# A linear-attention, soft-mixture and feed-forward kernel on one core: power table by ScalarE, query-key products on GpSimd, a shorter warm-up, and a new order of all units of the first stage

## The chip, the core and the metric

The kernel runs on one core of a Trainium2 chip. The metric is the device time in microseconds (us) of one execution. The engines named below are TensorE (PE in the profile, with PEld for its weight loads), VectorE (DVE), ScalarE (ACT), GpSimd (POOL) and SyncE (SP), which issues every DMA of this kernel.

## The reference

Three stages follow one another. The first is a recurrent linear attention over 768 steps, for 4 batches and 8 heads of width 48:

```
cur   = (u * k_t) outer v_t
y_t   = r_t @ (state + cur)
state = w * state + k_t outer v_t
```

The second is a soft mixture of experts on x of shape (3072, 384): logits = x @ phi (32 slots); a softmax over all tokens builds the slot inputs d.T @ x; eight experts apply relu(s @ w1[e]) @ w2[e] to four slots each; a softmax over the slots mixes the results back to the tokens. The third is a feed-forward layer on the result, relu(x @ w_in) squared, times w_out, with a hidden width of 2048. All values are float32; w_in and w_out arrive as 64-bit floats and are turned to 32 bits on the chip.

## The kernel before

The attention is done in 16 units. Unit n is batch n // 4 and a pair of heads n % 4; its 768 steps are six chunks of 128. Five buffers of 128 x 3072 hold the units (unit n lies in buffer n % 5); `load_unit(n)` fetches unit n once the unit five before it has been read for the last time.

Per unit, these steps are written, each a small helper:

- `decay(n, m)`: VectorE multiplies keys (m = 1) or queries (m = 0) by powers of w from a table `tabp` that lies in PSUM. EV and OD, a third argument in places, are the even and odd chunks.
- `turns(x, k)`: TensorE transposes for the keys of unit k (ScalarE copies them out to `kn`) and for the output of unit x.
- `A(n, par)`: TensorE products of keys and queries within the even or odd chunks, into two of three PSUM banks with the tag "A" (for unit 0 and par = 1, one of them is the bank `pp`).
- the diagonal of those products: for units 0 to 2 by `rk(n)` (key times query, on GpSimd) and `dg_of(n)` (TensorE sums), for later units by `pr1`, `pr2` (GpSimd) and `weigh` (VectorE). `diag` (GpSimd) spreads the diagonal into a tile, and `cp` (VectorE, two copies) puts the lower triangle of A beside it, which frees the two banks.
- `KV(n)`, `scan(n)`, `inter(n)`, `intra(n, par)`: the state of each chunk, its running sum (VectorE), and the two parts of the output. `L(n)` makes the logits, and `soft1a` to `soft4`, `both` and `c_max` to `c_div` are the softmax work of each batch.

The order of all these units is written out by hand as one list of some 380 calls, and each engine works through its own instructions in that order. So the list also fixes the order in SyncE's queue: an issue that waits holds up all issues behind it. Among the calls are the loads of the second stage's weights. `load_piece(j)` loads a third (512 KB) of one of the first eight weight matrices: w1 of experts 0 to 5, then w2 of experts 0 and 1; pieces 21 to 23 are w2 of expert 1. `load_weight(8)` to `(13)` load a whole matrix (1536 KB) into a buffer that the attention gives up: 8 to 11 need the buffers of units 11 to 14, 12 that of unit 15, 13 the buffer of `scan` and `kn`. `load_win(0)` loads the first quarter of w_in into the buffer that holds `xn` of batches 0 and 2, which `soft3(2)` reads last.

Ahead of the list stand the loads of units 0 to 4, six `keep_clock` calls on TensorE (12 matmul instructions with no result that is used), and the making of the table: VectorE copies w, squares it five times, takes reciprocals of the six powers in one instruction, and doubles the table six times. `filler(2)` is two more unused TensorE products.

Behind the list come the softmax of the last batch, the experts (`ups(a)` and `downs(a)`, two experts each; each `up` takes a bank with the tag "A"), and between them, on VectorE, the conversion of w_in and w_out: `conv_some` works on the quarters 0 and 1 of w_in once `ups(1)` has given up its buffer, and `wout_f32` works on w_out. VectorE then copies out parts of `soT`, with which the third stage begins. That stage's main loop is at line 1251.

Of the kernel before, what the change touches and what calls it, by code (L numbers as in the profile page):

```python
# [17 lines left out]
def rwkv_softmoe_ffn(ctx: ExitStack, tc: tile.TileContext, un, wt, ph, w1, w2, w_in, w_out, out):  # L18
# [185 lines left out]
    tabp = ps("tab")[:112].rearrange("p (a e) -> p a e", a=NP)  # L204
    neg, pos = pw[:, 0], pw[:, 1]
    nc.vector.memset(tabp[:, :, 64:65], 1.0)
    nc.vector.tensor_copy(pos[:, 0], base[:, :NP])
    for i in range(5):
        nc.vector.tensor_mul(pos[:, i + 1], pos[:, i], pos[:, i])
    nc.vector.reciprocal(neg[:, :6], pos[:, :6])  # L210
    nc.vector.tensor_copy(tabp[:, :, 63:64], neg[:, 0].unsqueeze(2))
    for i in range(6):
        n = 1 << i
        blk = tabp[:, :, 64 - 2 * n:64 + 2 * n].rearrange("p a (q x) -> p a q x", q=4)
        by = pw[:, :, i].rearrange("p s a -> p a s").unsqueeze(3).to_broadcast([112, NP, 2, n])
        nc.vector.tensor_tensor(blk[:, :, 0::3], blk[:, :, 1:3], by, ALU.mult)
# [273 lines left out]
    def rsc_of():  # L490
        nc.vector.tensor_tensor(rsc, tabp, uw.unsqueeze(2).to_broadcast([112, NP, 128]), ALU.mult)
# [6 lines left out]
    def carry_of():  # L498
        nc.scalar.copy(carry[:, :, :, 1:], pos[:, 7].unsqueeze(2).unsqueeze(3).to_broadcast([112, NP, D, NC - 1]))
# [7 lines left out]
    def load_piece(j):  # L507
        load_weight(pieces[j][0], pieces[j][1:])
# [5 lines left out]
    def constants():  # L514
        nc.vector.reduce_sum(sel, ident.rearrange("p (q s) -> p s q", q=4).unsqueeze(1).to_broadcast([128, 4, NS, 4]), axis=AX.X)
        nc.vector.reduce_sum(rm, ident.rearrange("p (q e j) -> p e q j", q=4, e=E), axis=AX.XY)
        nc.gpsimd.memset(ones, 1.0)

    decay(0, 1, EV)
    load_piece(10)  # L520
    decay(0, 1, OD)
    carry_of()
    decay(0, 0, EV)
    rk(0, EV)
    decay(0, 0, OD)
    rk(0, OD, nc.vector)
    filler(2)
    turns(None, 0)
    A(0, 0)
    decay(1, 1)  # L530
    A(0, 1)
    KV(0)
    dg_of(0)
    diag(0, 1)
    filler(2)
    rsc_of()
    filler(2)
    decay(1, 0)
    filler(2)
    filler(2)  # L540
# [24 lines left out]
    decay(3, 0)
    cp(1, 1)
    diag(1, 0)
    cp(1, 0)
    load_unit(5)
    inter(1)  # L570
    KV(2)
    scan(2)
    pr1(3)
    intra(1, 0)
    constants()
    intra(1, 1)
    dg_of(2)
    diag(2, 0)
    load_unit(6)
    A(2, 0)  # L580
    turns(0, 3)
    load_piece(7)
    decay(4, 0)
    L(0)
    A(2, 1)
    cp(2, 0)
    inter(2)
    intra(2, 0)
# [24 lines left out]
    cp(3, 1)
    L(2)
    decay(5, 0)
    A(4, 0)
    inter(3)
    KV(4)
    weigh(4)
    diag(4, 0)  # L620
    decay(6, 1)
    scan(4)
    cp(4, 0)
    load_piece(3)
    intra(3, 0)
    intra(3, 1)
    A(4, 1)
    turns(3, 6)
    L(3)
    soft1d(0)  # L630
    pr2(5)
    weigh(5)
    diag(4, 1)
    A(5, 0)
    cp(4, 1)
    load_piece(15)
    diag(5, 0)
    pr1(6)
    decay(7, 1)
    cp(5, 0)  # L640
    pr2(6)
    load_unit(8)
    soft1a(0)
    soft1b(0)
    load_piece(4)
    inter(4)
    diag(5, 1)
    decay(7, 0)
    KV(5)
    scan(5)  # L650
    intra(4, 0)
    intra(4, 1)
    load_unit(9)
    A(5, 1)
    cp(5, 1)
    turns(4, 7)
    load_piece(17)
    pr1(7)
    weigh(6)
    decay(8, 0)  # L660
    both(0)
    c_max(0)
    A(6, 0)
    inter(5)
    intra(5, 0)
    diag(6, 0)
    cp(6, 0)
    KV(6)
    c_sub(0)
    diag(6, 1)  # L670
    load_piece(14)
    pr2(7)
    intra(5, 1)
    load_unit(10)
    decay(8, 1)
    A(6, 1)
    load_piece(2)
    turns(5, 8)
    load_piece(6)
    pr1(8)  # L680
# [20 lines left out]
    A(7, 1)
    turns(6, 9)
    L(6)
    weigh(8)
    A(8, 0)
# [12 lines left out]
    c_exp(0)
    intra(7, 1)
    decay(10, 0)  # L720
    c_sum(0)
    A(8, 1)
    cp(8, 1)
    weigh(9)
    load_piece(16)
    turns(7, 10)
    load_piece(0)
    L(7)
    A(9, 0)
    soft1a(1)  # L730
    inter(8)
    soft1b(1)
    KV(9)
    load_unit(12)
    decay(11, 1)
    load_piece(18)
    intra(8, 0)
    intra(8, 1)
    scan(9)
    KV(10)  # L740
    pr1(10)
    pr2(10)
    load_piece(11)
    diag(9, 0)
# [34 lines left out]
    inter(10)
    load_piece(22)  # L780
    intra(10, 0)
    pr2(12)
    intra(10, 1)
# [4 lines left out]
    soft1d(1)
    weigh(11)
    diag(11, 0)  # L790
    diag(11, 1)
    decay(13, 1)
    load_piece(19)
    cp(11, 0)
    decay(13, 0)
    load_piece(20)
    load_piece(9)
    cp(11, 1)
    load_weight(8)
    decay(12, 0)  # L800
    decay(14, 1)
# [3 lines left out]
    L(10)
    pr1(13)
    scan(12)
    inter(11)
    A(12, 0)
    pr2(13)  # L810
    intra(11, 0)
    weigh(12)
    diag(12, 0)
    diag(12, 1)
    KV(13)
    weigh(13)
    intra(11, 1)
    cp(12, 0)
    A(12, 1)
    turns(11, 14)  # L820
    decay(14, 0)
    L(11)
    cp(12, 1)
    load_weight(9)
    soft1a(2)
    A(13, 0)
    inter(12)
    intra(12, 0)
    pr1(14)
    intra(12, 1)  # L830
    soft1c(2)
    scan(13)
    load_weight(10)
    A(13, 1)
    diag(13, 0)
    decay(15, 1)
    soft1b(2)
    pr2(14)
    turns(12, 15)
# [10 lines left out]
    pr2(15)  # L850
    cp(13, 1)
    intra(13, 1)
    cp(14, 0)
    c_sub(1)
    KV(14)
    A(14, 1)
    turns(13, None)
    soft1d(2)
    load_weight(11)
    scan(14)  # L860
    decay(15, 0)
    c_exp(1)
    L(12)
    diag(14, 1)
    soft3(2)
    inter(14)
    A(15, 0)
    intra(14, 0)
    cp(14, 1)
    intra(14, 1)  # L870
    KV(15)
    A(15, 1)
    weigh(15)
    soft4(0)
    soft4(1)
    soft4(2)
    load_weight(13)
# [6 lines left out]
    cp(15, 0)
    diag(15, 1)
    scan(15)
    L(13)
    cp(15, 1)
# [434 lines left out]
```

## Time and profile before

| | us |
|---|---|
| median of 3 runs (373.4 to 373.82) | 373.75 |
| the profiled execution | 374.71 |
| its span, from the first to the last instruction | 373.0 |
| TensorE busy in that span | 365.9 (98%) |
| VectorE busy | 266.4 (71%) |
| ScalarE busy | 206.9 (55%) |
| GpSimd busy | 103.1 (28%) |
| chain of work that ended last, TensorE's share | 96% |

The attention takes the span up to about 113 us, the softmax of the last batch and the experts up to about 144 us, and the feed-forward layer the rest. A busy share is an average over all of these.

### The profile page before, as it was taken

The numbers are of one execution on the slowest core, as the hardware profiler recorded it, in microseconds if no ns is written. First come the engines' busy times: TensorE is split into PE (matmuls) and PEld (weight loads), VectorE is DVE, ScalarE is ACT, GpSimd is POOL, SyncE is SP. The second block draws the span as 40 slices with busy tenths as digits, with TensorE's granted clock in tenths as the row PEclk, the third lists the DMA queues.
The fourth block names the chain that finished last, engine by engine and source line by source line (L and its number), as shares of the span: only waits on it lengthen the run. The fifth ranks groups of instructions, "written<-read, shape, count | busy, mean of one in ns | idle before, by whom it ended". The sixth has DMA issues, their size and how long they took to land.

```text
span 373.0 us, 9092 instructions
## 1 busy us (share of the span) xinstructions
PE 365.9 (98%) x3716; PEld 297.8 (80%) x3716; DVE 266.4 (71%) x459; ACT 206.9 (55%) x447; POOL 103.1 (28%) x117
## 2 busy tenths in 40 slices
PE   8999999999999999999999999999999999999995
PEld 6888878887987556787878888888888888888884
DVE  7979878878673695999785767556666766556663
ACT  3234534544445344988887765555555655555553
POOL 4658795595734131352222400000000000000000
PEclk9999999999999999999999999999999999999999
DMA  7999899999999998333322003000000220000004
GB/s 251 405 377 415 294 401 386 390 372 393 317 397 410 386 417 293 94 112 94 106 93 65 7 38 131 2 1 0 3 0 0 88 84 0 2 1 0 2 0 169
DMA packets 22665, 65.22 MB, mean 175 GB/s; under 512 B 2544, under 2 KB 4832, under 8 KB 22624
## 3 DMA queue, kind: packets, MB, share of 16 engines
q1 hardware_dynamic: 22624, 64.65, 46.6%
q8 instruction: 29, 0.48, 0.5%
q14 instruction: 12, 0.10, 0.1%
HBM read 59.00 MB, written 4.72 MB: 171 GB/s over the span
## 4 chain that ended last, share of the span: by engine, by line
PE 96%; ACT 1%; DVE 1%; issue 1%; POOL 0%; POOLq 0%; ACTq 0%
PE ps_A L1251 26%; PE ps_tab L1251 9%; PE ps_kv L1251 9%; PE ps_lg L1251 9%; PE ps_A L311 7%; PE ps_YO L341 3%; PE ps_YE L350 3%; PE ps_YO L1138 3%; PE ps_A L952 3%; PE ps_YO L350 3%; PE ps_tab L973 3%; PE ps_YE L1138 3%; PE ps_lg L364 2%; PE ps_kv L323 2%; PE ps_YE L274 2%; PE ps_lg L227 1%
## 5 line engine op out<-in xcount | busy, mean ns | idle before, releaser
L1162 DVE TENSOR_TENSOR slot<-slot,slot 128x512 fp32r<-128x512 f32 (+1 forms) x97 | 70.2, 725 | 53.8 <-PE ps_A L1251 18.5
L1251 PE MATMUL ps_A<-slot,slot 128*128 128x512 f32 x429 | 105.3, 389 | 0.0
L1251 PEld LDWEIGHTS ps_A<-slot,slot 128*128 128x128 f32 x429 | 80.4, 188 | 16.8 <-DVE slot L1162 0.2
L1159 ACT CAST slot<-slot 128x512 fp32r<-128x512 f32 x95 | 58.9, 620 | 49.2 <-DVE slot L1156 48.9
L1156 DVE TENSOR_TENSOR slot<-slot 128x512 f32<-128x512 f32 x69 | 47.6, 691 | 11.4 <-ACT slot L1149 11.2
L1251 PE MATMUL ps_tab<-slot,slot 128*128 128x512 f32 x144 | 55.6, 393 | 0.1
L1251 PE MATMUL ps_kv<-slot,slot 128*128 128x512 f32 x144 | 55.1, 390 | 0.0
L1251 PE MATMUL ps_lg<-slot,slot 128*128 128x512 f32 x144 | 55.1, 389 | 0.0
L316 DVE COPY_PREDICATED AT<-mask,ps_A 128x384 f32<-128x384 int32 x63 | 33.5, 584 | 8.5 <-PE ps_A L311 3.2
L1149 ACT ACTIVATE slot<-ps_YO 128x512 f32<-128x512 f32 (+1 forms) x49 | 28.8, 589 | 12.8 <-PE ps_YO L1138 12.3
L1149 ACT ACTIVATE slot<-ps_YE 128x512 f32<-128x512 f32 x48 | 28.7, 598 | 12.3 <-PE ps_YE L1138 11.7
L1017 POOL TENSOR_TENSOR slot<-wf,slot 128x384 fp32r<-128x384 f32 x16 | 19.9, 1246 | 52.8 <-ACT slot L1012 52.8
L300 POOL TENSOR_SCALAR_AFFINE_SELECT AT<-dg 128x768 f32<-128x768 f32 x32 | 28.1, 882 | 20.2 <-DVE dg L293 7.9
L1251 PEld LDWEIGHTS ps_tab<-slot,slot 128*128 128x128 f32 x144 | 27.0, 188 | 6.5 <-issue 0.6
L1251 PEld LDWEIGHTS ps_kv<-slot,slot 128*128 128x128 f32 x144 | 27.0, 188 | 5.7
L311 PE MATMUL ps_A<-slot 48*128 48x128 f32 x378 | 30.8, 289 | 0.7 <-issue 0.7
L1251 PEld LDWEIGHTS ps_lg<-slot,slot 128*128 128x128 f32 x144 | 27.0, 188 | 5.5
L241 DVE TENSOR_TENSOR slot<-slot,ps_tab 112x768 f32<-112x768 f32 (+1 forms) x34 | 29.8, 891 | 0.0
L311 PEld LDWEIGHTS ps_A<-slot 48*128 48x128 f32 x378 | 24.8, 187 | 5.8 <-issue 3.2
L289 POOL TENSOR_TENSOR slot<-slot,slot 128x576 f32<-128x576 f32 x13 | 18.4, 1419 | 8.7 <-ACT slot L281 8.7
L353 ACT COPY xT<-ps_YE 112x384 f32<-112x384 f32 x16 | 7.7, 480 | 23.4 <-PE ps_YE L350 23.4
L1138 PE MATMUL ps_YO<-slot,slot 128*128 128x512 f32 x48 | 18.8, 392 | 0.0
(223 smaller groups left out, 569.8 us busy)
## 6 DMA issues: line engine op xcount, KB each, us to landing
slot<-in_un_dram SPq DMA_DIRECT2D x12, 1344.0 KB, 8.2
slot<-in_w_dram SPq DMA_DIRECT2D x24, 512.0 KB, 9.2
slot<-in_w_dram SPq DMA_DIRECT2D x8, 1536.0 KB, 9.0
slot<-in_w_in_dram SPq DMA_DIRECT2D x4, 1536.0 KB, 8.7
wo<-in_w_out_dram SPq DMA_DIRECT2D x16, 384.0 KB, 3.3
out_dram<-slot SPq DMA_DIRECT2D x18, 256.0 KB, 2.1
slot<-in_un_dram SPq DMA_DIRECT2D x9, 448.0 KB, 6.9
slot<-slot SPq DMA_DIRECT2D x56, 16.0 KB, 1.8
```

What stands on the lines that cost most here:

```text
L241: nc.vector.tensor_tensor(x, x, t.unsqueeze(1).to_broadcast(list(x.shape)), ALU.mult)
L300: nc.gpsimd.affine_select(out=at, in_=dg.unsqueeze(3).to_broadcast([128, 2, HC, 128]), pattern=[[0, 2], [0, HC], [1, 128]], compare_op=ALU ...
L311: nc.tensor.matmul(p[h][:, i], tv[rows, 1, 2 * i + par], tv[rows, 0, 2 * i + par], start=True, stop=True)
L316: nc.vector.copy_predicated(st[n, "AT", par][:, h], mask.unsqueeze(1).to_broadcast([128, HC, 128]), p)
L350: nc.tensor.matmul(p[o:o + D, i], vv[:, 2 * i + par, h], at[:, h, i], start=False, stop=True, skip_group_check=True)
L1017: nc.gpsimd.tensor_tensor(wout_half(wls, f, 5), st.pop(("wf", f)), hi, ALU.subtract)
L1138: nc.tensor.matmul(p, gst[:, 128 * f:128 * (f + 1)], cTall[:, 512 * g:512 * (g + 1)], start=True, stop=True)
L1149: nc.scalar.activation(fs[i, "hr"][:, c], fs[i, "p"][:, c], AF.Relu)
L1156: nc.vector.tensor_mul(gg, hr, hr)
L1159: nc.scalar.copy(part(i, "gh")[:, c], fs[i, "gg"][:, c])
L1162: nc.vector.tensor_tensor(part(i, "gl")[:, c], fs[i, "gg"][:, c], fs[i, "gh"].bitcast(F32)[:, c], ALU.subtract)
L1251: nc.tensor.matmul(o, (hi, lo, hi)[k][:, 128 * j:128 * (j + 1)], (gh, gh, gl)[k], start=(f == 0 and k == 0 and i > 0), stop=(f == NF - 1 a ...
```

## The change

1. The table. The five squares move from VectorE to ScalarE, as Square activations. VectorE takes the reciprocals in three instructions, each ahead of the doubling that needs it, and starts from w itself; GpSimd makes the copy of w. The Exp activation that stood ahead of everything follows the squares.
2. `keep_clock(6)` becomes `keep_clock(4)`.
3. For unit 0 both halves of `rk` run on GpSimd (the odd half was VectorE's). For unit 1 the odd half runs on VectorE, and GpSimd keeps the even half.
4. All units of the list stand in a new order. The same calls are made, apart from `rk`. The pieces of weights come later, `load_weight(11)`, `(12)` and `(13)` come ahead of `load_win(0)`, and `load_piece(21)` comes last of all.

```diff
-    nc.scalar.activation(warm[:, 0:1], warm[:, 1:2], AF.Exp)
...
-    nc.vector.tensor_copy(pos[:, 0], base[:, :NP])
     for i in range(5):
-        nc.vector.tensor_mul(pos[:, i + 1], pos[:, i], pos[:, i])
-    nc.vector.reciprocal(neg[:, :6], pos[:, :6])
-    nc.vector.tensor_copy(tabp[:, :, 63:64], neg[:, 0].unsqueeze(2))
+        nc.scalar.activation(pos[:, i + 1], pos[:, i] if i else base[:, :NP], AF.Square)
+    nc.scalar.activation(warm[:, 0:1], warm[:, 1:2], AF.Exp)
+    nc.gpsimd.tensor_copy(pos[:, 0], base[:, :NP])
     for i in range(6):
         n = 1 << i
+        if i == 0:
+            nc.vector.reciprocal(neg[:, 0], base[:, :NP])
+            nc.vector.tensor_copy(tabp[:, :, 63:64], neg[:, 0].unsqueeze(2))
+        elif i in (1, 3):
+            nc.vector.reciprocal(neg[:, i:3 * i // 2 + 2], pos[:, i:3 * i // 2 + 2])
...
-    keep_clock(6)
+    keep_clock(4)
```

The head of the new order, with the calls that use TensorE, VectorE or GpSimd:

```
carry_of  decay(0,1,OD)  decay(0,1,EV)  decay(0,0,OD)  filler(2)  filler(2)
rk(0,OD)  A(0,1)  turns(None,0)  decay(0,0,EV)  rk(0,EV)  rsc_of  A(0,0)
decay(1,1)  decay(1,0)  KV(0)  dg_of(0)  diag(0,1)  scan(0)  filler(2) x3
diag(0,0)  cp(0,1)  turns(None,1)  filler(2)  cp(0,0)  UT_of  inter(0)
rk(1,EV)  rk(1,OD,nc.vector)  dg_of(1)  diag(1,1)  load_piece(10)  intra(0,0) ...
```

The head of the order before:

```
decay(0,1,EV)  load_piece(10)  decay(0,1,OD)  carry_of  decay(0,0,EV)  rk(0,EV)
decay(0,0,OD)  rk(0,OD,nc.vector)  filler(2)  turns(None,0)  A(0,0)  decay(1,1)
A(0,1)  KV(0)  dg_of(0)  diag(0,1)  filler(2)  rsc_of  filler(2)  decay(1,0)
filler(2) x2  scan(0)  cp(0,1)  turns(None,1)  ones_of  filler(2)  UT_of
diag(0,0)  cp(0,0)  inter(0)  rk(1)  dg_of(1)  diag(1,1)  intra(0,0) ...
```

TensorE's units around 82 us and in the tail, before (upper) and in the new order (lower):

```
soft3(1) L(10) inter(11) A(12,0) intra(11,0) KV(13) intra(11,1) A(12,1) turns(11,14) L(11)
soft3(1) L(10) inter(11) intra(11,0) intra(11,1) KV(13) A(12,1) turns(11,14) A(12,0) L(11)

L(12) soft3(2) inter(14) A(15,0) intra(14,0) intra(14,1) KV(15) A(15,1) turns(14) L(13) L(14) inter(15) intra(15,0) intra(15,1) L(15)
L(12) L(13) A(15,0) inter(14) KV(15) intra(14,0) intra(14,1) A(15,1) turns(14) soft3(2) inter(15) intra(15,0) intra(15,1) L(14) L(15)
```

SyncE's issues from the last unit on, before (upper) and in the new order (lower):

```
u15 p13 p19 p20 p9 w8 w9 w10 win0 w11 w13 w12
u15 p19 p20 p14 p23 p7 w8 w9 p16 p9 p13 w10 w11 w12 w13 win0 p21
```

Here u is `load_unit`, p is `load_piece`, w is `load_weight` and win0 is `load_win(0)`. Ahead of u15 the old order has 20 pieces and the new one 15.

## Rows read from the trace of the kernel before

**Rows 1.** The page, part 1: busy time and share of each engine.
```profile
PE 365.9 (98%) x3716; PEld 297.8 (80%) x3716; DVE 266.4 (71%) x459; ACT 206.9 (55%) x447; POOL 103.1 (28%) x117
```
**Rows 2.** Windows: stretch, length; busy us per engine; granted clock, DMA share, GB/s.
```profile
10.00:20.00 10.00, 9.59 (x230) 8.58 (x230) 9.08 (x14) 3.31 (x12) 7.17 (x9) 1.00 1.03 414
20.00:40.00 20.00, 20.00 (x464) 17.62 (x462) 17.50 (x30) 8.51 (x29) 14.20 (x15) 1.00 0.97 371
```
**Rows 3.** The chain that ended last: start us, us, what.
```profile
1.44 5.24 PE ps_lg L227 x12
...
10.53 1.98 PE ps_lg L231 x16
...
82.23 0.66 issue
...
109.08 1.00 PE ps_lg L364 x24
...
118.17 5.32 PE ps_A L952 x96
...
126.97 2.58 PE ps_tab L973 x32
```
**Rows 4.** Timeline of VectorE, 2 to 8 us: start, duration, instructions.
```profile
2.52 0.17 DVE L207 COPY slot<-base 112x4 f32<-112x4 f32 x1 [0.23 <-DMA base<-in_wt_dram]
2.73 0.96 DVE L209 TENSOR_TENSOR slot<-slot 112x4 f32<-112x4 f32 x5
3.73 0.30 DVE L210 RECIPROCAL slot<-slot 112x24 f32<-112x24 f32 x1
...
4.26 1.69 DVE L216 TENSOR_TENSOR ps_tab<-ps_tab,slot 112x8 f32<-112x8 f32 x6
5.99 1.95 DVE L241 TENSOR_TENSOR slot<-slot,ps_tab 112x384 f32<-112x384 f32 x4
```
**Rows 5.** Timeline of TensorE: the last `keep_clock` matmul and the first fillers.
```profile
6.29 0.39 PE L227 MATMUL ps_lg<-ident 128*128 128x256 f32 x1
6.51 0.61 PE L231 MATMUL ps_lg<-ident 128*128 128x128 f32 x4
```
**Rows 6.** Timeline of GpSimd and VectorE: the two halves of `rk(0)`.
```profile
7.55 1.00 POOL L479 TENSOR_TENSOR slot<-slot 112x384 f32<-112x384 f32 x1 [3.23 <-DVE slot L241]
7.97 0.99 DVE L479 TENSOR_TENSOR slot<-slot 112x384 f32<-112x384 f32 x1
```
**Rows 7.** DMA issues at 1.72 and 2.67 us (units 0, 1): KB, us to landing.
```profile
slot<-in_un_dram SPq DMA_DIRECT2D x1, 448.0 KB, 4.3
...
slot<-in_un_dram SPq DMA_DIRECT2D x1, 448.0 KB, 5.6
```
**Rows 8.** Timeline of SyncE's queue, 104 to 113 us (L149 win0; L193 weights 11, 13, 12).
```profile
104.45 0.37 SPq L149 DMA_DIRECT2D slot<-in_w_in_dram  x1
107.46 5.32 SPq L193 DMA_DIRECT2D slot<-in_w_dram  x3
...
111.00 0.38 SPq L193 DMA_DIRECT2D slot<-in_w_dram  x1
```
**Rows 9.** DMA issues of weights 10, 13, 12 (100.78, 111.00, 112.40 us): KB, us to landing.
```profile
slot<-in_w_dram SPq DMA_DIRECT2D x1, 1536.0 KB, 7.9
...
slot<-in_w_dram SPq DMA_DIRECT2D x1, 1536.0 KB, 8.8
...
slot<-in_w_dram SPq DMA_DIRECT2D x1, 1536.0 KB, 11.2
```
**Rows 10.** Timeline of VectorE, 123 to 145 us: conversions, then copies of `soT`.
```profile
123.55 0.43 DVE L156 TENSOR_SCALAR slot<-slot 128x512 int32<-128x512 int32 x1 [4.72 <-PE ps_A L952]
...
137.14 0.35 DVE L156 TENSOR_SCALAR wf<-wo 128x384 int32<-128x384 int32 x1
...
141.29 0.35 DVE L156 TENSOR_SCALAR wf<-wo 128x384 int32<-128x384 int32 x1
...
143.98 0.29 DVE L1088 COPY slot<-ps_A 128x128 f32<-128x128 f32 x1 [2.34 <-PE ps_A L1087]
```

More of the change, by code (lines that the diff above doesn't have):

```diff
@@ L517, in constants @@
         nc.gpsimd.memset(ones, 1.0)
+    carry_of()
+    decay(0, 1, OD)
     decay(0, 1, EV)
-    load_piece(10)
-    decay(0, 1, OD)
-    carry_of()
+    decay(0, 0, OD)
+    filler(2)
+    filler(2)
+    rk(0, OD)
+    A(0, 1)
+    turns(None, 0)
     decay(0, 0, EV)
     rk(0, EV)
[L525 to L528, printed above, removed]
+    rsc_of()
     A(0, 0)
     decay(1, 1)
-    A(0, 1)
+    decay(1, 0)
     KV(0)
@@ L570, in rwkv_softmoe_ffn @@
     inter(1)
+    rk(2)
+    pr1(3)
+    dg_of(2)
+    diag(2, 1)
+    intra(1, 0)
     KV(2)
     scan(2)
-    pr1(3)
-    intra(1, 0)
-    constants()
     intra(1, 1)
-    dg_of(2)
-    diag(2, 0)
     load_unit(6)
@@ L618, in rwkv_softmoe_ffn @@
     KV(4)
+    pr2(4)
+    decay(5, 0)
+    load_unit(7)
+    cp(3, 1)
     weigh(4)
@@ L621, in rwkv_softmoe_ffn @@
     decay(6, 1)
-    scan(4)
[L623 to L627, printed above, removed]
+    pr1(5)
+    decay(6, 0)
+    intra(3, 0)
+    diag(4, 1)
+    intra(3, 1)
+    cp(4, 0)
+    A(4, 1)
+    pr2(5)
+    scan(4)
+    cp(4, 1)
+    weigh(5)
+    decay(7, 0)
+    decay(7, 1)
     turns(3, 6)
     L(3)
[L630 to L633, printed above, removed]
+    soft1a(0)
+    diag(5, 0)
     A(5, 0)
-    cp(4, 1)
-    load_piece(15)
-    diag(5, 0)
+    inter(4)
+    load_piece(2)
@@ L638, in rwkv_softmoe_ffn @@
+    intra(4, 0)
+    load_piece(5)
     pr1(6)
-    decay(7, 1)
+    load_piece(6)
+    diag(5, 1)
+    load_unit(8)
     cp(5, 0)
     pr2(6)
-    load_unit(8)
-    soft1a(0)
+    KV(5)
+    intra(4, 1)
+    scan(5)
     soft1b(0)
[L645 to L653, printed above, removed]
     A(5, 1)
-    cp(5, 1)
     turns(4, 7)
[L657 to L660, printed above, removed]
     both(0)
-    c_max(0)
@@ L663, in rwkv_softmoe_ffn @@
     A(6, 0)
     inter(5)
+    cp(5, 1)
+    constants()
     intra(5, 0)
-    diag(6, 0)
-    cp(6, 0)
[L668 to L680, printed above, removed]
-    L(4)
-    L(5)
+    pr1(7)
+    KV(6)
+    load_piece(8)
+    weigh(6)
+    load_unit(9)
+    intra(5, 1)
+    diag(6, 0)
+    decay(8, 1)
+    pr2(7)
+    A(6, 1)
+    load_piece(15)
@@ L698, in rwkv_softmoe_ffn @@
     pr2(8)
-    scan(7)
+    turns(6, 9)
+    weigh(8)
+    L(6)
+    A(8, 0)
     diag(7, 1)
[L701 to L705, printed above, removed]
+    soft4(0)
     diag(8, 0)
-    inter(7)
-    intra(7, 0)
     cp(7, 1)
     decay(10, 1)
-    pr2(9)
-    diag(8, 1)
-    soft1c(0)
+    inter(7)
     KV(8)
     cp(8, 0)
-    decay(9, 0)
-    scan(8)
-    c_exp(0)
[L719 to L731, printed above, removed]
-    soft1b(1)
[L733 to L744, printed above, removed]
+    intra(7, 0)
+    intra(7, 1)
+    A(8, 1)
+    load_piece(17)
+    pr2(9)
+    scan(8)
+    turns(7, 10)
+    weigh(9)
+    load_unit(11)
+    soft1d(0)
+    diag(8, 1)
+    load_piece(4)
+    load_piece(18)
+    decay(10, 0)
@@ L745, in rwkv_softmoe_ffn @@
+    L(7)
+    cp(8, 1)
+    soft1a(1)
+    A(9, 0)
+    decay(11, 1)
+    diag(9, 0)
+    inter(8)
+    c_sub(0)
+    KV(9)
+    intra(8, 0)
+    scan(9)
+    load_unit(12)
+    intra(8, 1)
+    pr1(10)
+    KV(10)
+    pr1(11)
+    cp(9, 0)
+    load_piece(11)
+    load_unit(13)
+    load_piece(22)
+    c_exp(0)
+    soft1b(1)
+    load_piece(3)
     A(9, 1)
     diag(9, 1)
-    cp(9, 0)
-    load_unit(13)
+    soft1c(1)
     turns(8, 11)
+    cp(9, 1)
+    pr2(10)
+    weigh(10)
+    diag(10, 0)
@@ L776, in rwkv_softmoe_ffn @@
+    L(8)
     L(9)
     A(11, 0)
-    scan(11)
[L779 to L783, printed above, removed]
+    cp(10, 1)
+    inter(10)
+    soft1d(1)
+    intra(10, 0)
+    intra(10, 1)
+    decay(12, 0)
+    cp(11, 0)
+    pr1(13)
+    scan(11)
+    KV(12)
+    load_piece(12)
+    diag(11, 1)
     load_unit(15)
-    KV(12)
-    load_piece(13)
+    load_piece(19)
+    decay(13, 1)
+    pr1(12)
     A(11, 1)
[L788 to L795, printed above, removed]
-    load_piece(20)
[L797 to L801, printed above, removed]
+    cp(11, 1)
+    load_piece(20)
     turns(10, 13)
     soft3(1)
-    c_div(0)
[L805 to L820, printed above, removed]
@@ L821, in rwkv_softmoe_ffn @@
-    decay(14, 0)
[L822 to L839, printed above, removed]
+    c_max(1)
+    decay(13, 0)
+    load_piece(14)
+    scan(12)
+    c_sum(0)
+    pr2(12)
+    weigh(12)
+    L(10)
+    inter(11)
+    intra(11, 0)
+    intra(11, 1)
+    load_piece(23)
+    decay(14, 1)
@@ L840, in rwkv_softmoe_ffn @@
+    pr2(13)
+    load_piece(7)
+    load_weight(8)
+    weigh(13)
+    diag(12, 0)
+    KV(13)
+    diag(12, 1)
+    A(12, 1)
+    cp(12, 1)
+    turns(11, 14)
+    A(12, 0)
+    cp(12, 0)
+    L(11)
+    soft1a(2)
+    diag(13, 0)
+    c_div(0)
+    inter(12)
+    pr1(14)
+    c_sub(1)
+    scan(13)
+    A(13, 0)
+    pr1(15)
+    decay(14, 0)
     diag(13, 1)
     cp(13, 0)
+    c_exp(1)
+    load_weight(9)
+    intra(12, 0)
+    KV(14)
+    intra(12, 1)
+    A(13, 1)
+    load_piece(16)
+    load_piece(9)
@@ L842, in rwkv_softmoe_ffn @@
+    load_piece(13)
+    decay(15, 1)
+    cp(13, 1)
+    load_weight(10)
+    load_weight(11)
+    soft1b(2)
+    turns(12, 15)
+    pr2(14)
+    weigh(14)
+    diag(14, 0)
     both(2)
+    pr2(15)
     A(14, 0)
-    weigh(14)
-    pr1(15)
-    diag(14, 0)
+    decay(15, 0)
+    cp(14, 0)
+    load_weight(12)
     inter(13)
     intra(13, 0)
-    load_win(0, take(NSLOT, I32))
[L850 to L857, printed above, removed]
@@ L858, in rwkv_softmoe_ffn @@
-    soft1d(2)
[L859 to L871, printed above, removed]
-    A(15, 1)
[L873 to L877, printed above, removed]
+    intra(13, 1)
+    weigh(15)
+    load_weight(13)
+    A(14, 1)
+    diag(14, 1)
+    cp(14, 1)
+    turns(13, None)
+    load_win(0, take(NSLOT, I32))
+    scan(14)
+    L(12)
+    L(13)
@@ L878, in rwkv_softmoe_ffn @@
+    A(15, 0)
+    diag(15, 0)
+    diag(15, 1)
+    cp(15, 0)
+    soft4(1)
+    soft1c(2)
+    inter(14)
+    KV(15)
+    intra(14, 0)
+    intra(14, 1)
+    soft1d(2)
+    scan(15)
+    A(15, 1)
     turns(14, None)
-    load_weight(12)
-    diag(15, 0)
     c_max(2)
     c_sub(2)
+    soft3(2)
+    inter(15)
+    intra(15, 0)
+    cp(15, 1)
     c_exp(2)
[L884 to L888, printed above, removed]
+    intra(15, 1)
+    soft4(2)
     L(14)
     c_sum(1)
+    load_piece(21)
@@ L891, in rwkv_softmoe_ffn @@
     c_div(1)
-    inter(15)
     c_sum(2)
     c_div(2)
-    intra(15, 0)
-    intra(15, 1)
     L(NU - 1)
```

106 lines of the change are left out of this document (48 added, 58 removed).

## The prediction

> **What bounds the kernel now.** I read the page's busy shares first: TensorE is busy 98% of the span, the next engine 71% [rows 1]. A busy share can hide waits, so the windows and the chain of waits come next. From 20 to 40 us TensorE is busy the whole stretch [rows 2], and the chain runs through TensorE alone; in the whole attention after 20 us the largest piece that is not an engine's work is one "issue" of 0.66 us at 82.23 us [rows 3]. So in the middle of the attention the order of the units cannot make TensorE's own work shorter; it can only remove that wait or open new ones. Room is left at two places. The first is the start: TensorE spends 5.24 us on warm-up products and 1.98 us on fillers at 10.5 us [rows 3], while VectorE is busy 9.08 of the 10 us from 10 to 20 [rows 2]. There VectorE sets the pace. The second is the seam at 123 to 144 us, where VectorE converts weights and the feed-forward layer waits for its copies. I therefore read VectorE's timeline there, and SyncE's queue with the landings of its loads, because the change reorders that queue.
>
> **The table.** Today the copy of w starts at 2.52 us, when w lands, the squares at 2.73, the reciprocals at 3.73 and the doublings at 4.26; the first decay starts at 5.99 [rows 4]. The doublings thus hold 1.73 us. After the change VectorE keeps these, and ahead of or between them one reciprocal and one copy (0.2 each, the spacing of the small instructions of that timeline) and two more reciprocals of 8 and 12 columns (0.22 and 0.25, between the 0.2 of the smallest instructions and the 0.30 of 24 columns). That is 2.6 us, and the table is done at 5.1, so 0.88 us earlier. ScalarE's five squares are not in the trace of before. At VectorE's 0.2 each they end at 3.5, and the last reciprocal needs them at about 3.8; at 0.3 each they would end at 4.0 and cost 0.2. I take nothing. GpSimd's copy of w is one small instruction that the first doubling needs at 2.9; nothing too.
>
> **The first products.** Three half decays of 0.49 [rows 4] end at 6.57. The third reads the queries, whose chunk was issued at 1.72 and landed 4.3 us later [rows 7], at 6.0; it starts at 6.1, so the data just make it. A(0,1) starts at 6.6, where today the first real TensorE work follows the fillers at 7.12 [rows 5]: 0.5 us. The keys of unit 1 land at 8.27 (2.67 + 5.6 [rows 7]); that decay then leads by 0.6 us, not 0.88.
>
> **The warm-up.** The 12 matmuls of 256 columns take 5.24 us, 0.437 each [rows 3]. That is the lower clock level (1.2 GHz): the last of them took 0.22 (6.29 to 6.51), and the 128-column fillers behind it 0.11 [rows 5], which is the upper level (2.4 GHz), though the profile prints a granted clock of 1.00 throughout [rows 2]. Eight matmuls end at 4.94; the two filler calls moved up to follow them are eight instructions, 0.22 each at the lower level. If the clock rises again at about 6.3 us, six of them reach 6.3 and two more 6.5. TensorE then has no hole before A(0,1). So the four removed matmuls, 1.75 us, give back only what VectorE's earlier table lets through. Bounds of the gain of the start: 0.5 (first product) and 1.75 (the matmuls).
>
> **The rk products.** GpSimd's half takes 1.00; VectorE's took 0.99, running beside it from 7.97, against 0.49 for a decay of the same shape [rows 4, 6]. Both halves of unit 0 on GpSimd, one after the other from 6.6, end at 8.6; KV(0) ends at about 9.8, so TensorE does not wait for them. For unit 1, VectorE's half comes behind cp(0,0), at about 13.65 us; at 0.99 it ends at 14.65, some 0.2 after TensorE reaches dg_of(1). Following TensorE through fillers, turns, UT_of and inter with that, intra(0,0) starts some 0.9 us earlier than now. I take 0.9 for the start: nearer to VectorE's 0.88 than to the removed 1.75, as VectorE sets the pace.
>
> A rule of the Trainium skill bears on the last product ("SBUF — State Buffer", section "Who interferes with whom"): a VectorE instruction with two SBUF inputs and a GpSimd instruction that reads SBUF exclude each other, and the second waits until the first ends. Rows 6 agree: VectorE's product started inside GpSimd's and ended 0.41 us after it. By the rule the product of unit 1, which starts after GpSimd's half has ended, would take about 0.45 instead of 0.99; the start would then gain 1.05 to 1.1 instead of 0.9.
>
> **The middle.** The kinds of call and their number stay the same, and TensorE changes as often between its kinds. The 0.66 us wait stands ahead of A(12,1), behind KV(13): A(12,0) has taken two of three banks shortly before, and they come free with cp(12,0). In the new order A(12,1) comes first and turns(11,14) stands between the two, which should hide it. Against this, some 380 calls in a new order on a VectorE that is busy 17.5 of 20 us [rows 2] can open a wait of the same kind elsewhere. Bounds: a gain of 0.66, a loss of 1.0 (one and a half such waits). I take a gain of 0.3.
>
> **The loads.** SyncE issues in order, so a blocked issue holds what is behind it. Today win0 goes out at 104.45, and the weights 11, 13 and 12 at 107.46, 111.00 and 112.41, the last when unit 15 has been read [rows 8]. In the new order win0 and piece 21 stand behind 12 and 13. Unit 15 is read 0.9 us earlier through the start, and 0.5 earlier because L(14), half of the 1.00 us of the two L at 109.08 [rows 3], moves behind it: weight 12 goes out at 111.0. A 1536 KB load landed 7.9 us after its issue at best, and 8.8 with one just ahead of it; 13 and 12 landed at 119.8 and 123.6, 3.8 apart [rows 9]. So weight 12 lands at 118.9, 13 at 122.7, win0 at 126.5, and piece 21, a third of the size, at 127.8.
>
> **Who waits for them.** VectorE's first conversion today waits for TensorE until 123.55 [rows 10]; with the earlier start that is 122.65. Now it must wait for win0, until 126.5: 3.85 us late, and everything behind it in VectorE's order is as late, w_out's conversions at 137.14 and 141.29 and then the copies of soT. Ahead of that copy VectorE stands idle for 2.34 us today [rows 10]; that cover is used up, and 1.5 us are left on the path, since the feed-forward layer starts from soT. Piece 21 is needed by down(1), the second half of the 2.58 us at 126.97 [rows 3], at 128.26 - 0.9 = 127.4: a wait of 0.4, alongside the 1.5 and not added to it. Bounds of the late load: with 8.8 for weight 12 it is 2.4; if win0 landed by 125.0, nothing.
>
> **The sum.** -0.9 (start) - 0.3 (middle) + 1.5 (late win0) = +0.3 us. On the profiled execution, 374.71 (span 373.0 and 1.7 around it), that is 375.0. The median of the runs is 373.75, 0.96 below the profiled one, so I forecast 374.05 for it. A measurement of this kernel tells about 0.2% from no change, 0.75 us.
>
> **Rivals.**
> - Slower, by the same mechanism at a higher price. From a win0 that lands after 126.95 the loss exceeds 0.75 us. For it: 15 pieces are issued ahead of unit 15 where 20 were, so more bytes are left for the end, and 8.8 was usual behind another load. Against: weight 12 waits for unit 15 in any case, and by then the queue should be nearly empty. With 8.8 and no gain in the middle: -0.9 + 2.4 = +1.5, 375.25.
> - Faster: win0 does not hold VectorE beyond its idle 2.34 us. For it: an idle DMA queue might deliver the three matrices closer than 3.8 us apart. Against: rows 9. Then the start counts in full, with the middle's 0.3 to 0.66: -1.2 to -1.56, 372.2 to 372.55. It decides from a landing of win0 before 125.0.
> - The start does not give what it says: the clock rises later behind the shorter warm-up, and A(0,1) and the first turns run at the lower level; some 0.5 of the 0.9 is lost. With the late win0: -0.4 - 0.3 + 1.5 = +0.8, 374.55. Against: eight fillers keep TensorE busy to 6.3 us.
>
> **How the numbers follow.** Gains and late load nearly cancel: 0.41. Late load at a higher price, or a new wait on top: 0.27. Start lost: 0.07. Late load hidden: 0.25. So faster 0.25, same 0.41, slower 0.34. The likeliest case alone spans 373.0 to 374.5. The range has to take in both signs: down to 372.4 (most of the hidden case), up to 375.7 (the higher price with 0.45 of new waits).
>
> **What would show it.** Right: the first decay at about 5.1 us and A(0,1) at 6.6; eight warm-up matmuls, and fillers that speed up at about 6.3; in SyncE's queue win0 behind the weights 12 and 13, issued at about 112; VectorE's first conversion held by a DMA, not by TensorE; no idle time ahead of the soT copy. Wrong: win0 issued well before 111, a first conversion near 122.6, TensorE waits of over 0.5 us between 20 and 110, or cold matmuls after 7 us.

## The result and the profile after

| | before | after |
|---|---|---|
| median of 6 runs, us (lowest to highest) | 373.57 (373.09 to 373.82) | 377.52 (376.13 to 384.89) |
| the profiled execution, us | 374.71 | 377.43 |
| its span, us | 373.0 | 375.7 |

The ratio of the times is 1.0095, with an interval of 1.0077 to 1.0114; the run of 384.89 was disturbed and is left out of it. The kernel became slower by nearly 1%, and 377.5 lies above the forecast range (372.4 to 375.7).

Page, part 1 (against [rows 1]):

```profile
PE 366.3 (97%) x3712; PEld 297.1 (79%) x3712; DVE 266.1 (71%) x455; ACT 207.3 (55%) x452; POOL 100.5 (27%) x119
```

No engine's busy time grew by more than 0.4 us. The 2.7 us of span are in the main waiting, so they have to be found in the chain of waits (against [rows 3]; start, duration, what):

```profile
1.72 4.57 DMA slot<-in_un_dram
6.31 0.56 DVE slot L244
6.94 1.96 POOL slot L482 x2
8.90 1.88 issue
...
24.33 0.87 PE ps_A L314 x12
...
112.48 15.86 DMA slot<-in_w_in_dram
128.46 0.44 DVE slot L155
...
146.62 0.21 DVE slot L1092
```

Before, 96% of the chain was TensorE, from the first matmul to the end. Now it begins with the load of unit 0 and two GpSimd products, and between 112 and 147 us it consists almost wholly of one transfer, win0, and the VectorE conversions behind it. (The 1.88 us behind the products are not GpSimd's work: its timeline has it idle until ScalarE has copied the sums of `dg_of(0)`, which TensorE starts at 9.91.) SyncE's queue shows why (against [rows 8]; L192 is a whole weight, L148 is w_in, L195 a piece):

```profile
100.78 11.65 SPq L192 DMA_DIRECT2D slot<-in_w_dram  x4
112.48 0.48 SPq L148 DMA_DIRECT2D slot<-in_w_in_dram  x1
113.00 1.00 SPq L195 DMA_DIRECT2D slot<-in_w_dram  x1
```

Before, win0 went out at 104.45; now it does at 112.48. The DMA issues at 111.53 (weight 12), 112.00 (weight 13), 112.48 (win0), 113.00 (piece 21) and 124.52 us (first rows of w_out), with KB and us from issue to landing (against [rows 9]):

```profile
slot<-in_w_dram SPq DMA_DIRECT2D x1, 1536.0 KB, 8.9
...
slot<-in_w_dram SPq DMA_DIRECT2D x1, 1536.0 KB, 12.7
...
slot<-in_w_in_dram SPq DMA_DIRECT2D x1, 1536.0 KB, 15.9
...
slot<-in_w_dram SPq DMA_DIRECT2D x1, 512.0 KB, 16.6
...
wo<-in_w_out_dram SPq DMA_DIRECT2D x1, 384.0 KB, 17.2
```

Issue plus time to landing gives 120.4, 124.7, 128.4 and 129.6 us, and 141.7 for w_out (136.9 before). VectorE's timeline has the waits that follow (against [rows 4, 6, 10]; the bracket is the idle time ahead and what ended it):

```profile
5.06 1.02 DVE L244 TENSOR_TENSOR slot<-slot,ps_tab 112x384 f32<-112x384 f32 x2
6.31 1.02 DVE L244 TENSOR_TENSOR slot<-slot,ps_tab 112x384 f32<-112x384 f32 x2 [0.23 <-DMA slot<-in_un_dram]
...
8.67 0.95 DVE L244 TENSOR_TENSOR slot<-slot,ps_tab 112x768 f32<-112x768 f32 x1 [0.74 <-DMA slot<-in_un_dram]
...
13.61 0.53 DVE L482 TENSOR_TENSOR slot<-slot 112x384 f32<-112x384 f32 x1
...
16.06 1.82 DVE L244 TENSOR_TENSOR slot<-slot,ps_tab 112x768 f32<-112x768 f32 x2 [1.05 <-DMA slot<-in_un_dram]
...
128.46 0.43 DVE L155 TENSOR_SCALAR slot<-slot 128x512 int32<-128x512 int32 x1 [10.20 <-DMA slot<-in_w_in_dram]
...
146.54 0.48 DVE L1092 COPY slot<-ps_A 128x128 f32<-128x128 f32 x2
```

The table is ready when it was forecast (first decay at 5.06), but from 6 us on VectorE stands idle for loads, which it did nowhere between 6 and 18 us before. At the seam the first conversion starts at 128.46 instead of 123.55, which is 4.91 late. The 2.34 us that VectorE stood idle ahead of the first soT copy are used up, and 4.91 - 2.34 = 2.57 remain: the copy starts 2.56 late (146.54 for 143.98), and the span is 2.7 longer. In these two executions the seam holds nearly the whole loss. TensorE's timeline at three places:

```profile
5.00 1.74 PE L234 MATMUL ps_lg<-ident 128*128 128x128 f32 x8
6.92 0.37 PE L314 MATMUL ps_A<-slot 48*128 48x128 f32 x1 [0.18 <-DVE slot L244]
...
129.60 1.50 PE L977 MATMUL ps_tab<-slot,hT 128*32 128x384 f32 x16 [1.91 <-DMA slot<-in_w_dram]
```

And the windows from 10 to 60 us (columns as in [rows 2]; the last is GB/s), with the one from 40 to 60 us of before as the last line:

```profile
10.00:20.00 10.00, 9.37 (x224) 8.19 (x226) 8.47 (x13) 3.35 (x12) 6.43 (x7) 1.00 1.03 406
20.00:40.00 20.00, 19.61 (x455) 17.16 (x454) 16.09 (x26) 8.17 (x28) 13.15 (x12) 1.00 0.82 297
40.00:60.00 20.00, 19.82 (x397) 16.79 (x400) 17.73 (x30) 8.99 (x29) 15.55 (x18) 1.00 0.93 343
...
40.00:60.00 20.00, 19.70 (x401) 16.59 (x394) 15.53 (x26) 9.39 (x31) 15.36 (x14) 1.00 0.97 365
```

From 20 to 40 us the DMA engines moved 297 GB/s where they moved 371 before, and from 40 to 60 us 343 where it was 365. That is 20 us x 74 GB/s + 20 us x 22 GB/s = 1.9 MB less: the pieces that now come later. Summed over windows of 4 us, the shortfall has grown to 2.8 MB at 88 us. From 88 to 112 us every such window shows 396 to 419 GB/s, so the queue has hardly any room left, and at 112 us 1.6 MB are still missing, about 3.9 us at 413 GB/s. This debt is not made good before the last loads.

### The profile page after: what moved, and what is told of

Same layout as the page of the kernel before. It is cut to its first block, busy times and chain, and to the rows that moved or that the text cites. A ratio compares the mean times of both kernels' runs of the same rounds, so it can differ in the third digit from the quotient of the medians.

```text
span 375.7 us, 9072 instructions
## 1 busy us (share of the span) xinstructions
PE 366.3 (97%) x3712; PEld 297.1 (79%) x3712; DVE 266.1 (71%) x455; ACT 207.3 (55%) x452; POOL 100.5 (27%) x119
## 4 chain that ended last, share of the span: by engine, by line
PE 85%; DMA 5%; DVE 5%; issue 1%; ACT 1%; POOL 1%; SPq 0%; DVEq 0%; POOLq 0%; ACTq 0%
PE ps_A L1255 26%; PE ps_tab L1255 9%; PE ps_kv L1255 9%; PE ps_lg L1255 9%; PE ps_A L314 7%; DMA slot<-in_w_in_dram 4%; PE ps_YE L353 3%; PE ps_YO L344 3%; PE ps_YO L1142 3%; PE ps_YE L1142 3%; PE ps_YO L353 3%; PE ps_lg L367 2%; PE ps_YE L277 2%; PE ps_kv L326 2%; DMA slot<-in_un_dram 1%
## 5 line engine op out<-in xcount | busy, mean ns | idle before, releaser
L1166 DVE TENSOR_TENSOR slot<-slot,slot 128x512 fp32r<-128x512 f32 (+1 forms) x97 | 71.0, 733 | 55.0 <-PE ps_A L1255 18.5
L1021 POOL TENSOR_TENSOR slot<-wf,slot 128x384 fp32r<-128x384 f32 x16 | 17.1, 1069 | 56.0 <-ACT slot L1016 56.0
```

Of the source, the lines that this page charges most:

```text
L1166: nc.vector.tensor_tensor(part(i, "gl")[:, c], fs[i, "gg"][:, c], fs[i, "gh"].bitcast(F32)[:, c], ALU.subtract)
```

## The experiments

The first theory was that of the forecast: win0 in a later place of the queue costs the time. The rivals: the later pieces leave a debt of bytes; the new start costs instead of giving; TensorE's wait for piece 21 sets the end. The twelve kernels below "after" were timed in five rounds, in three groups, each against the kernel before on the same chip (medians 374.05, 374.21 and 374.31); the line "after" is the result above, against 373.57. "A(2,0)" and "soT" are starts in the profiled execution (TensorE's and VectorE's timelines). "Low clock" counts the runs whose mean granted clock was below 0.997, out of all runs.

| kernel | median us | ratio [interval] | A(2,0) | soT | low clock |
|---|---|---|---|---|---|
| before | 374.05 to 374.31 | | 23.71 | 143.98 | 3 of 95 |
| after | 377.52 | 1.0095 [1.0077, 1.0114] | 24.25 | 146.54 | 3 of 6 |
| e1_win0_ahead | 376.54 | 1.0052 [1.0025, 1.0078] | 25.72 | 145.81 | 3 of 12 |
| e2_piece21_early | 378.68 | 1.0108 [1.0073, 1.0143] | 24.21 | 145.74 | 5 of 8 |
| e3_pieces_as_before | 375.63 | 1.0045 [1.0012, 1.0079] | 25.89 | 146.14 | 3 of 12 |
| e4_pieces_and_win0 | 374.76 | 1.0031 [1.0003, 1.0058] | 24.63 | 143.80 | 3 of 12 |
| e5_dg2_late | 375.80 | 1.0044 [1.0019, 1.0069] | 24.38 | 144.45 | 3 of 12 |
| s1_table | 374.00 | 1.0011 [0.9989, 1.0033] | 23.93 | 143.30 | 2 of 12 |
| s2_table_clock4 | 374.43 | 1.0002 [0.9981, 1.0023] | 23.13 | 143.66 | 0 of 12 |
| h1_old_head | 374.30 | 1.0007 [0.9984, 1.0030] | 23.11 | 142.15 | 1 of 12 |
| h2_pieces_earlier | 374.45 | 1.0012 [0.9996, 1.0028] | 22.72 | 143.00 | 2 of 12 |
| m1_new_middle | 374.26 | 1.0007 [0.9993, 1.0021] | 23.61 | 143.26 | 1 of 12 |
| x1_old_with_new_loads | 377.53 | 1.0097 [1.0071, 1.0123] | 24.18 | 146.05 | 3 of 6 |
| x2_old_with_new_head | 375.48 | 1.0045 [1.0027, 1.0063] | 24.09 | 144.34 | 2 of 12 |

**win0 ahead of weight 12**, all else as after:

```diff
+    load_win(0, take(NSLOT, I32))
     load_weight(12)
...
-    load_win(0, take(NSLOT, I32))
```

> The changed kernel with one call moved: win0 is issued ahead of weight 12 (behind 11), so it no longer waits for unit 15; piece 21 stays last. Theory 'place in the queue': win0 lands near 120 us, VectorE converts from about 122.9 us as TensorE allows, and 2.6 us come back (about 374.7). Theory 'bytes late': the pieces put later have left some 6 us of transfers for the end, so the first w_out rows still land near 141.7 us; VectorE then waits for those instead, and only about 1 us comes back (about 376.3). Theory 'order of the units': nothing comes back.

About half of the loss came back. In its VectorE timeline the first conversion no longer waits for a DMA, but the first one of w_out does:

```profile
124.45 0.43 DVE L155 TENSOR_SCALAR slot<-slot 128x512 int32<-128x512 int32 x1 [4.73 <-PE ps_A L956]
...
141.93 0.36 DVE L155 TENSOR_SCALAR wf<-wo 128x384 int32<-128x384 int32 x1 [3.75 <-DMA wo<-in_w_out_dram]
```

The bytes that are owed moved the wait from win0 to w_out. The order of the queue is not the whole cause.

**Piece 21 early**, behind piece 7:

```diff
     load_piece(7)
+    load_piece(21)
...
-    load_piece(21)
```

> The changed kernel with only piece 21 moved, to right behind piece 7. TensorE's wait of 1.9 us ahead of down(1) goes. If that wait set the time, 1.9 us come back (about 375.4). If VectorE's late conversion sets it, nothing does (377.3, within 0.5).

TensorE's wait at the second half of `down` (1.91 us in after) is gone, and the time is no better. The median lies above both expected values; five of the eight runs are at low clock, and the other three (376.33 to 377.40) lie where those of after do (376.13 to 377.43). That wait lies alongside VectorE's, as the prediction took it to.

**All pieces in their old places**, the tail of the queue as in after:

```diff
+    load_piece(1)
...
+    load_piece(7)
+    load_piece(5)
+    load_piece(8)
...   (and so on for all pieces)
```

> The changed kernel with the order of all 24 pieces against the unit loads as it was before (piece 21 among them); weights 8 to 13 and then win0 as in the change. Theory 'bytes late': the queue is empty when weight 12 is issued, win0 lands near 127.0 instead of 128.4 us, and 1.4 us come back (about 375.9). Theory 'place in the queue' alone: the same, as win0 still waits for unit 15. If neither holds, the time stays at 377.3.

Half of the loss came back here too, and win0 is still late:

```profile
128.07 0.43 DVE L155 TENSOR_SCALAR slot<-slot 128x512 int32<-128x512 int32 x1 [8.32 <-DMA slot<-in_w_in_dram]
```

Here the landings can be read with less owed. Weight 12 went out at 113.01 and landed 7.1 us later (8.9 in after), and win0 landed 15.0 us after that issue; in after it took 16.9, in the forecast 15.5. So 1.9 us of win0's delay in after go with the later pieces. (This profiled execution and that of e1 hold a fall of the clock at 22 us, told at the end, so their starts at A(2,0) and later are about 1.5 us late for that alone.)

**Both together**:

> Both: pieces ordered as before, and win0 ahead of weight 12. All loads of the seam land in time: win0 near 118 us, w_out near 138 us. If the loads are the whole loss, TensorE's lead of 0.57 us at the experts is kept: about 373.0, 0.15% below the kernel before. If the order of the units costs in itself, it stays above 374.5.

```profile
123.37 0.43 DVE L155 TENSOR_SCALAR slot<-slot 128x512 int32<-128x512 int32 x1 [4.72 <-PE ps_A L956]
...
143.80 0.29 DVE L1092 COPY slot<-ps_A 128x128 f32<-128x128 f32 x1 [1.55 <-PE ps_A L1091]
```

VectorE's timeline of this kernel has the seam of before again: the conversion waits for TensorE, and idle time stands ahead of the soT copy, which starts as early as before; a wait of 0.84 us for w_out, at 137.88, lies inside that cover. What is left of the loss in the time is 0.3%. The intervals of e1, e3 and e4 overlap, so it is the waits in the traces, and not the times, that tell place and debt apart. A(2,0) starts 0.92 us later than before, so the start was tried next.

**The new loads alone**: before, with nothing but its loads in the new order.

```diff
-    load_piece(10)      (all pieces to their new places)
...
-    load_win(0, take(NSLOT, I32))
...
+    load_weight(13)
+    load_win(0, take(NSLOT, I32))
+    load_piece(21)
```

> The kernel before, with only the order of the weight loads of the change: the pieces later, weights 11, 12 and 13 ahead of win0, piece 21 last. If the loads are the loss, they cost here as well: weight 12 is issued at 112.4 us, win0 lands near 129.3 us, VectorE's first conversion starts there instead of at 123.55, and 3 to 3.5 us are lost (about 377.2). If the new order of the compute units is what costs, the time is that of the kernel before.

Its ratio is that of the whole change, and its VectorE timeline shows the same wait:

```profile
127.94 0.43 DVE L156 TENSOR_SCALAR slot<-slot 128x512 int32<-128x512 int32 x1 [9.92 <-DMA slot<-in_w_in_dram]
```

With e4 this settles the main cause from both sides: the loads' order, late pieces and late win0 together, is enough for the loss, and without it two thirds of the loss are gone (0.31% for 0.95%). Among runs that are not at low clock, the median of e4 is 374.62 (nine runs), that of before beside it 374.13.

**The table alone, and with the shorter warm-up** (both: before, with that part of the change):

```diff
-    keep_clock(6)       (only in the second)
+    keep_clock(4)
```

> The kernel before with the new making of the table alone (squares on ScalarE, reciprocals step by step), six keep_clock calls and the old order kept. Theory 'VectorE sets the pace of the start': the table is 0.9 us earlier, the warm-up still holds TensorE to about 7 us, and 0.2 to 0.5 us are gained. Theory 'the landings of the first units set it': no gain (within 0.2).

> As the run beside it, with four keep_clock calls. If the shorter warm-up is harmless, TensorE starts on unit 0 at about 6.2 us and 0.5 to 0.9 us are gained against the kernel before. If the shorter warm-up makes the clock fall to the lower level again in some executions (seen at 22.4 to 25.7 us in two profiles of variants of the change), several runs show a mean granted clock of 0.991 to 0.996 and are 1.5 us or more longer.

Neither changes the time. With six `keep_clock` calls TensorE comes to A(2,0) no earlier, since the warm-up holds it; with four it is 0.58 earlier, but at up(0) only 0.33 of that is left (117.77 for 118.10), for a wait of 0.6 at `inter` opened on the way.

**dg_of(2) and diag(2,1) behind intra(1,1)**, on top of e4:

```diff
-    dg_of(2)
-    diag(2, 1)
     intra(1, 0)
     KV(2)
     scan(2)
     intra(1, 1)
+    dg_of(2)
+    diag(2, 1)
```

> The changed kernel with the loads mended and dg_of(2) put back behind intra(1,1); the rest of the new head stays. The 0.39 us wait of dg_of(2) goes. If that wait, amid products of two columns, lets the clock fall at 22 us, all runs keep a mean clock of 0.998 or more. If the warm-up or the wait of intra(0,0) at 15 to 16 us does it, a quarter of the runs still fall.

TensorE's 0.39 us wait ahead of KV(2) is gone, and nothing is gained: three of the 12 runs are still at low clock, `dg_of(2)` now waits 0.35 us for VectorE's scan, and the chain runs through GpSimd's `diag` (24.83) and VectorE's copy (26.54) to A(2,1), which starts at 27.18 where after had it at 26.51.

**The new head alone**: before, with the new table, four `keep_clock` calls, the new order of the head to just behind A(2,0), and the new engines of `rk`.

```diff
-    decay(0, 1, EV) ... rk(0, OD, nc.vector)
+    carry_of() ... rk(0, OD)  A(0, 1)  turns(None, 0) ... rk(0, EV)
```

> The kernel before, with the change's table, four keep_clock calls, its rk engines and its list up to the first products of unit 2; loads and everything behind as before. If the new head gives its table's lead away (rk on GpSimd, dg_of(2) ahead of KV(2)), the products of unit 2 start at 24.3 to 24.7 us against 23.78, and 0.5 to 0.9 us are lost. If it also brings the falls of the clock, about a quarter of the runs show a mean clock below 0.997; of the kernel before, 3 of 66 did. If the head is as good as the old one with the new table, 0.5 us are gained.

Slower by 0.45%, though part of that is this kernel's own: I kept `constants()` near its old place, and in its chain of waits that work holds VectorE for 1.05 us, with TensorE waiting 1.0 us at A(2,1) behind it. In after it comes much later.

```profile
25.14 1.05 DVE sel L518
```

The rest is put down to the head: two waits of TensorE, 0.34 at 15.5 and 0.41 at 21.5 us, as in after. The losses of x1 and x2 add up to more than that of after (0.97% and 0.45% against 0.95%), which fits a landing that sets the end: behind it a later start costs little more.

**The old head on the new middle**, with the loads mended as in e4, the new table and four `keep_clock` calls:

> The changed kernel with the loads mended (pieces as before, win0 ahead of weight 12) and the list's head, up to the first products of unit 2, in the old order with the old engines for rk; table and four keep_clock calls as in the change. If the new head (rk on GpSimd, dg_of(2) ahead of KV(2)) is what lost the start, TensorE reaches the experts about 1 us earlier than before, and the time is 0.7 to 1.2 us below the kernel before, with no fall of the clock. If the shorter warm-up causes the falls of the clock, they stay, in a quarter of the runs.

Its profiled execution is the earliest of all up to the experts: up(0) at 116.27, 1.83 ahead of before, and 373.08 in all. The conversion of w_out then waits for its load:

```profile
138.10 0.36 DVE L155 TENSOR_SCALAR wf<-wo 128x384 int32<-128x384 int32 x1 [2.48 <-DMA wo<-in_w_out_dram]
```

It was issued at 120.89, ahead of e4's (122.54) by just the lead that TensorE has over e4 at up(0) (1.65), yet the conversion begins at 138.10 where e4's began at 137.88. The DMA has become the bound there. In this execution the wait still fits into VectorE's idle time, and the soT copy keeps the lead (142.15 against 143.98), with no idle time left ahead of it. In the time no gain is seen: the runs lie between 373.08 and 378.07, and why most of them lose the lead is not shown, as only this one was profiled.

**The same with pieces one unit load earlier:**

```diff
+    load_piece(4)
     load_unit(...)
-    load_piece(4)       (likewise pieces 7, 17, 2, 21 and 13)
```

> A version meant to beat both: old head and rk engines, new table and four keep_clock calls, the new order behind it, win0 ahead of weight 12, and one or two pieces moved ahead by one unit load, into stretches in which the queue ran empty. Its sister with the pieces as before had TensorE at the experts 1.84 us early, but VectorE waited 2.5 us for w_out's first rows. If those rows land 1 us or more earlier here, the time is 1.2 to 1.8 us below the kernel before (372.3 to 372.9); if the queue is full all the way, no better than the sister.

The DMA wait at the first conversion of w_out has shrunk from 2.48 to 0.87 us, but TensorE waits 0.8 us at `inter` instead, and up(0) starts at 117.12.

**The new middle alone:** before up to A(2,0), the new order behind it, loads mended.

> The kernel before in everything up to the first products of unit 2 (old table, six keep_clock calls), then the new order of the compute units, with the loads mended. If the middle of the new order is worth what the traces say (the wait at 82 us gone, L(14) moved), TensorE reaches the experts near 116.9 us against 118.17, and the time is 0.6 to 1.2 us below the kernel before. If the middle is worth nothing, it is the same.

0.7 us earlier at the seam in the trace (first conversion 122.83 for 123.55), and no difference in the time. No kernel of the twelve measures faster than before.

## Why the prediction was wrong

**The mechanism was right, and it is the main part of the loss.** win0 behind the weights 12 and 13 (issued at 112.48, forecast "about 112"), a first conversion held by a DMA, no idle time left ahead of the soT copy: all as forecast. x1, in which the loads alone are changed, has nearly the same wait (9.92 us) and the same loss.

**The step that failed is the landing of win0** ("by then the queue should be nearly empty"; landing at 126.5). It landed at 128.4. Taken along the queue: weight 12 went out at 111.53 instead of 111.0 (0.5), took 8.9 instead of 7.9 (1.0), and weight 13 followed it by 4.3 instead of 3.8 (0.5). Weight 11 was still on its way until 116.2, and from weight 10 on (112.5, 116.2, 120.4, 124.7, 128.4) the landings form one train, some 4.0 us apart. The prediction had named the reason in its rival, 15 pieces ahead of unit 15 where there were 20, and set it aside because weight 12 must wait for unit 15 in any case. That is true of its issue; its landing depends on what is still owed at that moment. The size of it was to be had: of the five pieces more behind unit 15, four stand ahead of win0, 4 x 512 KB = 2.1 MB, which is 5.1 us at the 414 GB/s of [rows 2] and near the 1.9 MB that the windows from 20 to 60 us show. e3 is the check: with the pieces in their old places win0 landed 15.0 us after the issue of weight 12, where the forecast had 15.5 and after 16.9. The 5.1 us added in full would have been too much, though: when weight 12 went out, weight 11 needed another 4.7 us in after and still 3.1 in e3. What is owed at that issue is the better count: 4.7 and three landings 4.0 apart are 16.7, and 16.9 was measured. That rival had a chance of 0.27 with new waits added to it, and even it was priced at 375.25, with the 8.8 that the rows showed for one load ahead.

**The sum had an error of its own.** Where a landing sets the end, what TensorE gains ahead of it does not count, apart from what it moves the issue. By the prediction's own numbers the conversion would be 126.5 - 123.55 = 2.95 late and the copy 2.95 - 2.34 = 0.6; subtracting another 0.3 for the middle was wrong. The remainder closes: 0.3 forecast, 0.3 for this error, 1.9 for the later landing and 0.1 from landing to conversion are 2.6, and 2.56 was measured at the soT copy.

**The step from the profiled execution to the median failed too.** The prediction took 0.96 off its 375.0, since the profiled execution of before was that much slower than the median of its runs. After's profiled execution (377.43) lies 0.09 below its median (377.52), so 1.05 of the 3.47 us between forecast and measurement come from this term, and the other 2.4 from the sum above. Part of it may be the 0.66 us wait at 82 us, which only before's profiled execution has (below), and the low clock of three of after's six runs; this was not tested.

**The start: forecast 0.9 earlier, measured 0.5 later** (A(2,0) at 24.25 for 23.71). The table (5.06), eight warm-up matmuls and A(0,1) (6.92, forecast 6.6) went nearly as said, though this is 0.2 ahead of before's first real work and not 0.5. The false step was "VectorE sets the pace": once the table is early, VectorE waits for the loads of keys and queries, 0.23 for unit 0's queries, 0.74 and 0.40 for unit 1, 1.05 for unit 3. The new order makes this worse. It puts A(0,1), which needs the queries, first on TensorE, so that `dg_of(0)` starts at 9.91, hardly earlier than before (9.95), and the first `diag` at 10.81 for 10.84. In s2, with the same table and number of warm-up calls and the old order, `turns(None, 0)` stands first, needs the keys alone and starts at 6.00; there `dg_of(0)` starts at 8.95. The products of `rk(0)` on GpSimd end at 8.90 and are not what holds it. At `dg_of(1)` after is 0.48 ahead (14.71 for 15.19). Behind a wait of 0.34 at 15.6 almost nothing of that is left (A(1,0) at 19.57 for 19.61), and a wait of 0.39 at 21.7, inside `dg_of(2)`, makes up most of the 0.5. Across the kernels the order shows: with the new order of the head A(2,0) lies at 24.1 to 24.6 (five profiled executions at full clock), with the old order and old table at 23.6 to 24.2 (three), with the old order, new table and four `keep_clock` calls at 22.7 to 23.1 (three). So the table and the warm-up did give 0.6 to 1.0 at this place, and the new order took more than that back. In the time s2 shows that even that gain alone is not kept.

**The product on VectorE** took 0.53, not the 0.99 that I used, so the rule of the Trainium skill ("SBUF — State Buffer", "Who interferes with whom") gave the better price here. It brought no gain: TensorE waits 0.34 at 15.6 us all the same.

**The middle: forecast 0.3, seen 1.1, and the reason is not shown.** From A(2,0) to up(0) after took 93.28 us, before 94.39. But the 0.66 us wait at 82 us, on which the term rested, is absent also in the profiled executions of s1, s2, x1 and x2, which have the old order there; so the old order alone does not bring it. The five with the old middle order need 93.1 to 94.6 us for this stretch, the nine with the new one (after, e1 to e5, m1, h1, h2) 93.1 to 94.4, and m1 gives no gain in the time. A single wait of one profile was taken for a property of the order.

**Piece 21:** forecast a wait of 0.4, measured 1.91, beside the path both times (e2).

## What to carry to other kernels

When loads are moved within an in-order queue, count the bytes still owed when the last blocked issue goes out and divide by the full rate the windows show; the issue time of the load alone, plus its best latency, is too early. Put the load that is needed first ahead of those that must wait for a late release, and test order and debt both, since mending one only moves the wait to the next load (win0 to w_out here). Before a gain is booked for removing a wait, look whether the wait is there in a second execution, and whether what sets the end behind it is moved at all.

## What was not expected of the hardware

In some executions TensorE's granted clock falls to one half (1.2 of 2.4 GHz) in the middle of the start. The profiled execution of e1 shows it, in windows of 1 us (the column after the engines is the granted clock):

```profile
22.00:23.00 1.00, 1.00 (x28) 0.98 (x29) 0.00 (x0) 0.18 (x1) 0.36 (x1) 0.62 1.03 423
23.00:24.00 1.00, 1.00 (x21) 1.00 (x19) 0.00 (x0) 0.24 (x1) 0.66 (x2) 0.50 0.45 174
24.00:25.00 1.00, 1.00 (x22) 1.00 (x20) 0.37 (x1) 0.24 (x1) 0.71 (x1) 0.50 0.06 25
25.00:26.00 1.00, 1.00 (x12) 0.65 (x10) 1.00 (x2) 0.16 (x1) 0.00 (x0) 0.68 0.00 0
```

Just ahead of it TensorE did `dg_of(2)`, 48 products of two columns each, with a wait of 0.41 us inside. A(2,0) then starts at 25.72, 1.5 later than in after's profile. The profile of e3 has the same fall at the same place (A(2,0) at 25.89). It differs from run to run: in e1 the three runs of low clock have a median of 377.32, the nine others 375.42. Low clock is commonest in the three kernels in which pieces and win0 are both late (after, e2 and x1, 11 of 20 runs); it was seen in 14 of 60 runs of the others with the new head, in 6 of 60 of the others with the old head, and in 3 of 95 of before. So it may be a part of the average loss, by an estimate about half a microsecond (a quarter of the runs by some 2 us, as in e1), and of the 0.3% that e4 kept. Only the profiled executions of e1 and e3 have such a fall ahead of the last 6 us; where it lies in the other runs of low clock is not known. What sets it off is open: x2 has the same products and the same 0.41 us wait without a fall in its profile, e5 has no wait inside `dg_of(2)` and three runs of low clock in 12, the shorter warm-up alone (s2) had none in 12 runs, and x1, with the old head and six `keep_clock` calls, had three in 6.
